# Transposing softmax weights as f16 pairs in 32-bit elements, with a new start and a new order of all steps

## The chip, the cores and the metric

The kernel runs on one core of one Trainium2 chip. The metric is the device time of one execution in microseconds (us), taken over several runs. Beside the runs there is one profiled execution, whose instructions the trace lists with start and duration.

## What is computed

There are 8 batches and 8 heads, x has 512 rows of 64 numbers in each, and a state has 32 rows. Two attentions go between x and the state, their outputs are put side by side over the heads (8 x 64 = 512 columns), and a two-layer network with a PReLU runs over all 4,352 rows.

```
scores = scale * x @ state.T          # 512 x 32 per batch and head
a      = softmax(scores, -1);  xread = a @ state
scores2 = scale * state @ x.T         # 32 x 512
a2     = softmax(scores2, -1); sread = a2 @ x
rows   = concat([xread, sread], axis=2) -> (8 * 544, 512)
h = rows @ w_in                       # 512 -> 2048
g = max(h, 0) + alpha * min(h, 0)
out = g @ w_out                       # 2048 -> 512
```

(The reference's network reads rows x w_in of shape 512 x 2048 and w_out of shape 2048 x 512.)

## The kernel before

The kernel does not compute xread and then multiply by w_in. For each batch it makes m = state x w_in (steps `m` and `mo`: TensorE into PSUM, then a cast to f16 by ScalarE or VectorE), and the first layer is then h = a x m, taken transposed: `first` (step `F`, line 570) runs for each of 16 slices `jc` of 128 columns of w_in two matmuls of 128 x 512, one for each group `g` of four heads. Stationary is m, moving are the softmax weights `aT`, which `weights(b, g)` cuts out.

The weights come about as follows, for each batch b. `sc` (line 328) gives the scores in PSUM with heads and states on the partitions. `sb` (line 360) turns them by a VectorE transpose of 32 x 32 blocks, so that the 32 states of a softmax lie next to each other in one partition. Then come `smax` (393), `ssh` (398, subtract the maximum, POOL for batches 1 to 7), `sexp` (407, ScalarE), `ssum` (416, 417, sum and reciprocal), `snorm` (420, multiply and write f16 into `an`, on VectorE for batches 2 to 7, on POOL for batches 0 and 1) and `wb` (428, VectorE transpose back from `an` to `aT`). Batch 0 goes another way, in two halves j, with TensorE transposes: `xt`/`xo` transpose x, `tsc` (367) gives the scores with tokens on the partitions, and `at`/`ao` transpose the weights.

The other softmax, over tokens, has steps `tm` (440), `nb` (447), `te` (457), `tsum` (467) and `tn` (473 on ScalarE, 475 on POOL: scale e by the sum's reciprocal), then `tt` (a transposing DMA issued by SyncE), and `rd` (494) reads x with it.

After `F` come `N` (623, ScalarE: the negative part) and `G` (626, VectorE: PReLU into g). The second layer of batch 0 is `S` (640). Batches 1 to 7, and the sread rows of all batches as an eighth, use a scheme of seven block products instead of eight: `U` (708, POOL) makes sums and differences of blocks of g, `W` (684, POOL) those of w_out once, `P` (729) multiplies, `K` (745) keeps an intermediate result, `Q` (760, 762) adds and stores.

What sets the order is the text `ORDER`: a list of some 1,100 steps written out, each a name of the table `steps` with its arguments, for instance `F.1.7.1` (first layer, batch 1, slice 7, PSUM bank 1) or `tn.0.1.p` (scale e of batch 0, group 1, on POOL). Each engine runs its own instructions in this order; semaphores keep the dependencies. PSUM has eight banks; the banks 0 to 5 are named by tags `k0` to `k5`, and a step that names a bank waits until the last reader of the tile before it is done.

`Z` (`fill`, line 246) multiplies a pattern by itself and reads no result: it keeps TensorE busy while it would wait. Its count is in units of 256 columns, and each fill takes a tile of its own in the named bank. A first fill of 16 units is issued outside the order, before the first step.

The start, outside the order too: ScalarE issues the load of batch 0's states (line 189), and `load_x0` issues the five loads of batch 0's x (line 176), three by SyncE and two by ScalarE; POOL writes the pattern, the identity for transposes and zeros into `st_pairs`. POOL issues all later loads of x (`lx`), of states (`lst`) and of the network's weights (`wi`, `wo`).

Of the kernel before, what the change touches and what calls it, by code (L numbers as in the profile page):

```python
# [9 lines left out]
F16 = mybir.dt.float16  # L10
EXP = mybir.ActivationFunctionType.Exp
# [11 lines left out]
xt.1.0.1.3 at.0.4 ao.0.a xo.1.0.0.v snorm.p.0.1 Z.1.3 xo.1.0.1.v oma.a xo.1.1.1.v at.1.1 sc.1 f.0.0.0.3 ao.1.a wi.2  # L23
F.0.3.0 F.0.2.2 m.0.1.4.1 mo.2.0.a.0 Z.5.3 n.0.0.0 f.0.0.1.5 N.0.3 mo.0.1.a.0 sb.1 tm.1 mo.0.1.a.1 F.0.7.4 F.0.5.1
N.0.2 g.0.0.0.1 g.0.0.0.0 G.0.2 n.0.0.1 G.0.3 g.0.0.1.1 nb.1.a te.1.0 g.0.0.1.0 N.0.7 N.0.5 F.0.6.3 G.0.7 smax.1
S.0.0.0.2 G.0.5 te.1.1 F.0.4.0 S.0.0.1 S.0.3.1.5 wo.1 wi.3 S.0.3.0 tsum.1 N.0.6 m.0.2 mo.0.2.a wo.2 S.0.1.1.4 wo.3
W.1.0.p G.0.6 S.0.1.0 m.1.1 F.0.10.1 N.0.4 G.0.4 mo.1.1.a N.0.10 G.0.10 F.0.8.3 S.0.1.3 S.0.1.2 ssh.p.1 sexp.1 F.0.9.0
ssum.1.s N.0.9 lx.2 xd.2 S.0.0.3 N.0.8 G.0.8 F.0.11.1 N.0.11 S.0.3.3 W.1.1.p snorm.p.1 m.0.3 mo.0.3.a S.0.3.2 S.0.0.2
G.0.11 sc.0.1 sc.0.0 F.0.15.3 G.0.9 F.0.14.1 S.0.3.4 S.0.1.4 S.0.1.5 tm.0 tn.1.1.a tn.1.0.a tt.1 N.0.15 G.0.15 W.2.0.p
N.0.14 G.0.14 wb.1 nb.0.a W.4.0.p F.0.13.0 te.0.1 te.0.0 tsum.0 F.0.12.3 N.0.12 S.0.0.5 S.0.1.7 m.1.3 F.1.7.1 N.0.13  # L30
tn.0.1.p W.3.1.p W.3.0.p tn.0.0.a N.1.7 G.0.12 G.0.13 G.1.7 F.1.3.3 N.1.3 W.2.1.p S.0.0.7 mo.1.3.a S.0.1.6 O.0.1.v
W.4.1.p F.1.5.0 N.1.5 S.0.3.6 G.1.3 G.1.5 F.1.2.1 N.1.2 G.1.2 F.1.15.4 N.1.15 F.1.12.3 G.1.15 N.1.12 G.1.12 m.1.2
F.1.6.0 N.1.6 G.1.6 F.1.14.1 N.1.14 G.1.14 mo.1.2.a S.0.0.4 S.0.0.6 O.0.0.a F.1.0.4 N.1.0 F.1.13.3 sc.2 sb.2 m.2.2.0.1
mo.2.2.a.0 mo.2.2.a.1 tm.2 S.0.3.7 tt.0 smax.2 S.0.3.5 O.0.3.a N.1.13 S.0.2.1.2 nb.2.a S.0.2.5 te.2.1 S.0.2.6 S.0.2.7
te.2.0 F.1.1.0 N.1.1 G.1.13 F.1.8.1 N.1.8 G.1.0 G.1.1 F.1.4.5 S.0.2.2 m.3.2 G.1.8 N.1.4 G.1.4 rd.0.3 rd.1.4 F.1.10.0
lst.1 ssh.p.2 sexp.2 rdo.1.a mo.3.2.a ssum.2.1 tsum.2 S.0.2.4 S.0.2.0 F.1.9.5 lx.3 P.1.2.0.1.4 snorm.v.2 rdo.0.a N.1.9
G.1.9 S.0.2.3 N.1.10 P.1.1.0.1.3 P.1.1.1.1 P.1.2.1.1 O.0.2.a tn.2.0.a m.2.3.1.2 mo.2.3.a.0 m.2.1 mo.2.3.a.1 wb.2
G.1.10 F.1.11.5 N.1.11 mo.2.1.a G.1.11 P.1.1.1.0 U.1.1.1.p str.1.1 sro.1.v tn.2.1.p tt.2 F.2.15.2 F.2.1.0 xd.3
# [24 lines left out]
K.3.4.a nb.6.a te.6.0 F.4.0.0 N.4.0 U.3.3.1.p F.4.1.2 N.4.1 mo.6.3.a.0 P.3.3.0.1 te.6.1 P.3.7.1.0 U.3.4.0.p P.3.7.1.1
xd.7 smax.6 ssh.p.5 G.4.6 P.3.7.0.1 P.3.3.1.0 sexp.5 P.3.2.1.1.1 P.3.2.0.0 G.4.0 m.5.2 m.6.2.5.0 mo.6.2.a.1 ssh.p.6
sexp.6 mo.5.2.a U.4.1.1.p P.3.2.0.1 P.3.2.1.0 G.4.1 Q.3.1.1 ssum.5.2 Q.3.0.0 snorm.v.5 P.3.4.1.1 P.3.4.1.0 P.3.3.1.1
P.4.1.0.0.0 mo.6.2.a.0 P.3.3.0.0 Q.3.0.1.a P.4.1.0.1 P.4.1.1.1 P.3.4.0.0 P.4.1.1.0 wb.5 K.4.1.a m.7.2.1.5 mo.7.2.a.0
mo.7.2.a.1 m.5.1 tsum.6 P.4.2.1.0.3 mo.5.1.a P.4.2.1.1 ssum.6.2 P.3.4.0.1 Q.3.1.0 snorm.v.6 F.5.15.1 F.5.3.5 N.5.3
P.4.2.0.1 P.4.2.0.0 N.5.15 G.5.3 F.5.2.4 N.5.2 U.4.1.0.p U.4.2.0.p sc.7 G.5.15 F.5.0.2 N.5.0 G.5.2 G.5.0 F.5.7.5 N.5.7
G.5.7 U.4.2.1.p P.4.6.0.1 F.5.12.1 N.5.12 G.5.12 F.5.5.4 U.4.3.0.p F.5.9.2 N.5.5 G.5.5 N.5.9 G.5.9 P.4.6.1.1 F.5.10.5
P.4.6.0.0 tm.7 P.4.6.1.0 F.5.8.1 N.5.10 F.5.1.4 F.5.14.2 K.4.2.a N.5.14 Q.4.0.0 G.5.14 P.4.5.1.1 U.4.3.1.p P.4.5.1.0  # L70
P.4.5.0.0 G.5.10 nb.7.a wb.6 te.7.0 P.4.5.0.1 N.5.1 te.7.1 tsum.7 F.5.4.3 G.5.1 N.5.8 G.5.8 P.4.7.0.0.2 F.5.11.5
N.5.11 G.5.11 K.4.4.a tn.7.0.a P.4.7.0.1 P.4.7.1.1 P.4.7.1.0 F.5.6.4 N.5.6 U.4.4.1.p P.4.3.0.1 P.4.3.1.1 tn.6.1.p
F.6.2.1 N.6.2 U.4.4.0.p P.4.3.0.0 P.5.1.1.0.5 P.4.3.1.0 sb.7 Q.4.1.1 P.4.4.1.1 P.4.4.0.1 G.6.2 G.5.6 smax.7 P.4.4.0.0
P.4.4.1.0 tn.6.0.a Q.4.0.1.a Q.4.1.0 N.5.4 G.5.4 F.6.4.1 N.6.4 G.6.4 P.5.1.0.0 F.6.9.0 F.6.1.4 N.6.9 G.6.9 F.5.13.2
N.5.13 tt.6 tn.7.1.p G.5.13 F.6.5.3 N.6.5 G.6.5 U.5.1.0.p P.5.1.1.1 F.6.14.1 P.5.1.0.1 U.5.2.0.p ssh.p.7 F.6.3.0
F.6.12.2 N.6.14 G.6.14 P.5.2.0.1.3 P.5.2.1.1 tt.7 F.6.6.1 K.5.1.a P.5.6.0.0 P.5.6.1.0 P.5.2.1.0 N.6.3 G.6.3 N.6.1
# [25 lines left out]
def kernel(  # L102
# [56 lines left out]
    def load_x(b):  # L159
# [4 lines left out]
        )  # L164


    def load_x0():
        xgs[0] = att.tile([128, H, 2, 2, D], F16, name="xg_0", tag="xg", bufs=3)
        for j in range(2):
            t = att.tile([128, H, 2, D], F32, name=f"x0_{j}", tag="ts", bufs=2)  # L170
            x0s.append(t)
# [642 lines left out]
```

## Time and profile before

| | us |
|---|---|
| median of 3 runs | 209.11 |
| lowest and highest run | 208.97, 209.56 |
| span of the profiled execution, first to last instruction | 209.0 |

The time of the profiled execution as a whole is not listed apart from its span.

In the profile PE is TensorE's matmuls, PEld its loads of stationary operands, DVE VectorE, ACT ScalarE, POOL GpSimd and SP SyncE. A row of the grouped view has line, engine, operation, the tiles written and read, shapes and count; then the busy time of the group in us, the mean of one in ns, the idle time of the engine just ahead of them and what ended it. A row of a timeline begins with start and duration in us. In the view by stretches each row is one stretch of time; behind its bounds and its length stand busy us and the number of instructions for PE, PEld, DVE, ACT and POOL, then TensorE's granted clock as a share, the mean number of DMA engines' busy share and GB/s. A row of waits says who waited for what, the us in total, how often, and the longest. The chain of waits is the work that ended last, followed back from the last instruction. Matmuls are pipelined, and their ends are modelled.

### The profile page before, as it was taken

What the parts mean: (1) busy time and instruction counts of PE and PEld (TensorE: products, weight loads), DVE (VectorE), ACT (ScalarE), POOL (GpSimd) and SP (SyncE); (2) the same over time, 40 slices, a digit from 0 to 9 for tenths busy, and PEclk for the clock granted to TensorE, in tenths of its full rate; (3) what the DMA queues carried; (4) which work ended last, traced back from release to release, by engine and by line L of the source; (5) the groups of instructions that cost most, each with busy time, mean ns of one, the idle gap of its engine ahead of it and who ended that gap; (6) DMA issues with size and microseconds to landing.
All of it is one profiled execution on the core that took longest, in us unless ns stands there. A gap on an engine that the chain in (4) does not pass through costs nothing.

```text
span 209.0 us, 5033 instructions
## 1 busy us (share of the span) xinstructions
PE 201.8 (97%) x1997; PEld 134.8 (65%) x1997; DVE 171.7 (82%) x251; ACT 155.6 (74%) x306; POOL 179.7 (86%) x113
## 2 busy tenths in 40 slices
PE   7899999998999999999999999999999999999992
PEld 2554343345556666678667765786877687788882
DVE  0688989999899999999999999999996967733231
ACT  4489999999999999987989968868855757603120
POOL 8149589987999899997997999887997999999960
PEclk9999999999999999999999999999999999999999
DMA  6999997984956799219886630126101200023223
GB/s 170 215 204 161 193 205 102 201 117 85 198 133 74 125 184 174 53 11 161 231 122 86 153 118 32 53 78 174 51 4 52 84 18 3 0 100 104 100 75 126
DMA packets 44038, 23.68 MB, mean 113 GB/s; under 512 B 22256, under 2 KB 43504, under 8 KB 44016
## 3 DMA queue, kind: packets, MB, share of 16 engines
q1 hardware_dynamic: 31152, 14.82, 28.3%
q0 software_dynamic: 11792, 8.09, 27.5%
q10 hardware_dynamic: 1072, 0.46, 0.9%
q8 instruction: 15, 0.25, 0.5%
q14 instruction: 7, 0.06, 0.1%
HBM read 17.31 MB, written 8.91 MB: 125 GB/s over the span
## 4 chain that ended last, share of the span: by engine, by line
PE 78%; DMA 7%; POOL 6%; ACT 4%; DVE 2%; issue 1%; SPq 0%; POOLq 0%
PE px L729 24%; PE h L570 21%; PE pv L729 13%; PE py L729 6%; POOL ws L684 5%; PE m_ps L521 4%; PE h L579 3%; DMA e2T<-e 2%; DMA xT<-xg 2%; DMA x<-in_x_dram 2%; PE fill L246 2%; PE sr_ps L494 2%; PE o L640 1%; ACT m L545 1%; POOL an L420 1%; PE sc L328 1%
## 5 line engine op out<-in xcount | busy, mean ns | idle before, releaser
L626 DVE SCALAR_TENSOR_TENSOR g<-neg,oma_sb,h 128x512 f16<-128x512 f32 (+1 forms) x142 | 93.9, 709 | 11.9 <-ACT neg L623 11.4
L623 ACT ACTIVATE neg<-h 128x512 f32<-128x512 f32 (+1 forms) x142 | 75.7, 580 | 16.6 <-PE h L570 11.5
L570 PE MATMUL h<-aT,m 128*128 128x512 f16 x252 | 66.8, 379 | 0.1
L729 PEld LDWEIGHTS <-gsum 128*128 128x128 f16 x480 | 46.6, 98 | 13.0 <-issue 0.9
L729 PEld LDWEIGHTS <-g 128*128 128x128 f16 x360 | 34.9, 98 | 9.0 <-issue 1.4
L708 POOL TENSOR_TENSOR gsum<-g,g 128x1024 f16<-128x1024 f16 (+1 forms) x16 | 32.2, 2012 | 5.5 <-DVE g L626 3.7
L570 PEld LDWEIGHTS <-m 128*128 128x128 f16 x252 | 23.8, 98 | 18.1 <-issue 1.8
L708 POOL TENSOR_TENSOR gsum<-g,gsum 128x1024 f16<-128x1024 f16 (+1 forms) x16 | 32.1, 2008 | 1.5 <-PE px L729 1.0
L708 POOL TENSOR_TENSOR gsum<-gsum,g 128x1024 f16<-128x1024 f16 (+1 forms) x16 | 32.1, 2009 | 1.0
L729 PE MATMUL px<-ws,gsum 128*128 128x256 f16 x240 | 32.1, 273 | 0.0
L708 POOL TENSOR_TENSOR gsum<-g 128x1024 f16<-128x1024 f16 (+1 forms) x16 | 32.0, 2011 | 0.0
L745 ACT COPY kept<-px 128x512 f32<-128x512 f32 (+1 forms) x24 | 13.6, 567 | 21.0 <-PE px L729 20.9
L547 ACT CAST m<-m_ps 128x512 f16<-128x512 f32 x35 | 19.2, 602 | 1.8 <-PE m_ps L521 1.5
L762 DVE TENSOR_TENSOR oq<-pv,kept 128x512 f32<-128x512 f32 (+1 forms) x16 | 10.4, 649 | 10.6 <-PE pv L729 10.4
L398 POOL TENSOR_TENSOR ts<-ts,mx 128x1024 f32<-128x1024 f32 x7 | 13.3, 1912 | 5.3 <-DVE mx L393 5.3
L729 PE MATMUL px<-w_out_sb,gsum 128*128 128x256 f16 x120 | 17.2, 273 | 0.0
L729 PE MATMUL px<-w_out_sb,g 128*128 128x256 f16 x120 | 17.2, 273 | 0.0
L729 PE MATMUL py<-w_out_sb,g 128*128 128x256 f16 x120 | 16.6, 273 | 0.0
L640 PE MATMUL o<-w_out_sb,g 128*128 128x512 f16 x64 | 16.4, 379 | 0.0
L729 PE MATMUL pv<-ws,gsum 128*128 128x256 f16 x120 | 16.4, 273 | 0.0
L729 PE MATMUL pv<-ws,g 128*128 128x256 f16 x120 | 15.9, 273 | 0.0
L545 ACT CAST m<-m_ps 128x1024 f16<-128x1024 f32 x13 | 13.3, 1023 | 0.4 <-PE m_ps L521 0.3
(75 smaller groups left out, 241.3 us busy)
## 6 DMA issues: line engine op xcount, KB each, us to landing
out_dram<-oq SPq DMA_DIRECT2D x28, 256.0 KB, 2.6
xg<-in_x_dram POOLq DMA_DIRECT2D x7, 512.0 KB, 7.0
w_in_sb<-in_moe_w_in_dram POOLq DMA_DIRECT2D x4, 512.0 KB, 8.5
w_out_sb<-in_moe_w_out_dram POOLq DMA_DIRECT2D x4, 512.0 KB, 12.9
out_dram<-osb SPq DMA_DIRECT2D x4, 256.0 KB, 3.5
x<-in_x_dram SPq DMA_DIRECT2D x2, 256.0 KB, 3.9
out_dram<-oq SPq DMA_DIRECT2D x4, 128.0 KB, 2.1
x<-in_x_dram ACTq DMA_DIRECT2D x1, 256.0 KB, 4.7
```

Of the source, the lines that this page charges most:

```text
L398: engine(e).tensor_tensor(blocks(cols(live["ts", b], j, S)), blocks(scored(b, j)), over_blocks(cols(live["mx", b], j, S // N)), ALU.subtract,)
L545: copier(e)(m_tile(b, f), t)
L547: copier(e)(m_tile(b, f)[:, g, :], t[g])
L570: nc.tensor.matmul(h.rearrange("p (r j s) -> p r j s", r=2, j=2), ms[b, f][:, g, 128 * j : 128 * (j + 1)], weights(b, g), start=(g == 0), ...
L623: nc.scalar.activation(neg, h, RELU, bias=0.0, scale=-1.0)
L626: nc.vector.scalar_tensor_tensor(g_tile(b, jc), negs.pop((b, jc)), oma_sb[:, jc : jc + 1], hs.pop((b, jc)), ALU.mult, ALU.add,)
L640: nc.tensor.matmul(outs[b, q], g_tile(b, jc)[:, 128 * q : 128 * (q + 1)], w_out_sb[:, jc, :], start=not begun and jc == 2 * jc2, stop=left ...
L684: engine(e).tensor_tensor(ws[i][:, rows, :], w_halves[a][:, rows, :], (ws[b] if b in ws else w_halves[b])[:, rows, :], ALU.subtract,)
L708: engine(e).tensor_tensor(t, x(), y(), op)
L729: nc.tensor.matmul(pbanks[b, name][:, i, :], of(b, c)[:, j, 128 * i : 128 * (i + 1)], moving[:, 4 * c + j, :], start=not begun and j == 0, ...
L745: copier(e)(t, pbanks[b, "x"])
L762: nc.vector.tensor_tensor(osb, pbanks[b, name], kept[b, add], ALU.add)
```

## The change

1. `state_norm` writes `an` for batches 1 to 7 so that the two weights that lie 512 apart in the old order (r = 0 and 1) become neighbours, and `weights_back` reads and writes the tiles as 32-bit elements: one VectorE transpose of 128 x 512 elements of 4 bytes instead of 128 x 1024 of 2 bytes. `weights` then hands `first` every second f16.
2. The x of batch 0 is loaded by four DMAs of 256 KB, all issued by SyncE; ScalarE issues only the load of the first states. These loads, the pattern (128 columns wide instead of 256), the identity and the zeros of `st_pairs` become steps of the order: `dx`, `dst`, `io`, `id`, `mz`.
3. All fills write into one tile in bank 5 and count in units of 128 columns. There are 133 units, the first 36 ahead of the first transposes.
4. `ORDER` is written anew. Some steps change engines: of the scalings `tn`, 10 instead of 5 are on POOL; 7 of 24 copies `K` are on VectorE instead of ScalarE; likewise 3 of `nb`, 2 of `rdo`, one `ao`.

```diff
 ORDER = """
-lst.0 cx.0.1.v cx.0.0.a xt.0.0.0.0 stc.a stt.1 cx.1.0.v sbd.1.a sto.a sbd.0.a xt.0.0.1.2 xt.0.1.0.3 xo.0.1.0.a
-xo.0.0.0.v Z.4.3 xo.0.0.1.v tsc.0.1.4 cx.1.1.v tsc.0.0 smax.0.0 ssh.v.0.0 xt.0.1.1.5 xo.0.1.1.a sexp.0.0 tsc.1.0.0
-Z.1.9 tsc.1.1 str.0.1 wi.0 m.0.0.2.3 sro.0.a Z.5.6 smax.0.1 ssh.v.0.1 Z.5.6 m.2.0.5.4 lx.1 sexp.0.1 m.1.0 mo.0.0.a.0
-la mo.0.0.a.1 ssum.0.0 wi.1 mo.1.0.a ssum.0.1 wo.0 mo.2.0.v.1 snorm.p.0.0 xt.1.1.0.0 xt.1.0.0.1 xt.1.1.1.2 xo.1.1.0.a
...
+dx.0.1.s dx.0.0.s dx.1.1.s io cx.0.1.v dx.1.0.s lst.0 Z.5.36 dst.a id xt.0.0.1.3 cx.0.0.a stc.v stt.4 xt.0.0.0.0
+Z.5.11 cx.1.1.v Z.5.3 mz xo.0.0.0.v sbd.0.a xo.0.0.1.a xt.0.1.1.0 sbd.1.v cx.1.0.a tsc.0.0.1 tsc.0.1 Z.5.8 smax.0.0 la
+xt.0.1.0.3 sto.a xo.0.1.1.a Z.5.3 xo.0.1.0.v str.0.2 wi.0 tsc.1.0.3 lx.1 tsc.1.1 ssh.v.0.0 Z.5.5 Z.5.4 sro.0.a Z.5.9
+smax.0.1 m.0.0.1.4 m.2.0.2.0 sexp.0.0 m.1.0 ssh.v.0.1 mo.0.0.a.0 sexp.0.1 Z.5.4 ssum.0.0 wi.1 Z.5.26 wo.0 xt.1.1.0.1
+mo.0.0.a.1 mo.1.0.a xt.1.0.0.4 xo.1.1.0.a xt.1.0.1.3 mo.2.0.v.1 ssum.0.1 xt.1.1.1.0 wi.2 xo.1.0.1.a Z.5.5 mo.2.0.a.0
...
 """
...
-        for e, j, first, last in (
-            (nc.sync, 0, 0, 4), (nc.sync, 0, 4, 8), (nc.scalar, 1, 0, 4),
-            (nc.scalar, 1, 4, 6), (nc.sync, 1, 6, 8),
-        ):
-            e.dma_start(
-                x0s[j][:, first:last, :, :],
-                x[0, first:last, 256 * j : 256 * (j + 1), :].rearrange("k (p r) d -> p k r d", r=2),
-            )
...
+    def load_x0(j, g, e):
+        heads = slice(4 * g, 4 * g + 4)
+        issuer(e).dma_start(
+            x0s[j][:, heads, :, :],
+            x[0, heads, 256 * j : 256 * (j + 1), :].rearrange("k (p r) d -> p k r d", r=2),
+        )
...
     def fill(k, n):
-        t = single(k, f"fill_{len(zs)}", [128, 512], F32)
-        zs.append(t)
-        widths = [384] * 2 if n == 3 else [512] * (n // 2) + [256] * (n % 2)
-        for w in widths:
+        if "fill" not in live:
+            live["fill"] = single(k, "fill", [128, 512], F32)
+        for w in [4] * (n // 4) + ([n % 4] if n % 4 else []):
             nc.tensor.matmul(
...
-            )
-
-    zs = []
-    fill(0, 16)
...
     def state_norm(e, b, j=None):
-        engine(e).tensor_tensor(
-            blocks(cols(live["an", b], j, S)),
-            blocks(cols(live["ts", b], j, S)),
-            over_blocks(cols(live["r1", b], j, S // N)),
-            ALU.mult,
-        )
+        an = blocks(cols(live["an", b], j, S))
+        ts = blocks(cols(live["ts", b], j, S))
+        r1 = over_blocks(cols(live["r1", b], j, S // N))
+        if b:
+            an = live["an", b].rearrange("p (a n r) -> p r a n", n=N, r=2)
+            ts = ts.rearrange("p (r a) n -> p r a n", r=2)
+            r1 = r1.rearrange("p (r a) n -> p r a n", r=2)
+        engine(e).tensor_tensor(an, ts, r1, ALU.mult)

     def weights_back(b):
-        nc.vector.transpose(live["aT", b], live["an", b])
+        nc.vector.transpose(live["aT", b].bitcast(U32), live["an", b].bitcast(U32))

     def weights(b, g):
         if b == 0:
             aT = live["aT", b].rearrange("p (j r g s) -> p r j g s", j=2, r=2, g=2)
         else:
-            aT = live["aT", b].rearrange("p (r j g s) -> p r j g s", j=2, r=2, g=2)
+            aT = live["aT", b].rearrange("p (j g s r) -> p r j g s", j=2, r=2, g=2)
         return aT[:, :, :, g, :]
```

More of the change, by code (lines that the diff above doesn't have):

```diff
@@ L10 @@
 F16 = mybir.dt.float16
+U32 = mybir.dt.uint32
 EXP = mybir.ActivationFunctionType.Exp
@@ L24 @@
[L24 to L38, printed above, removed]
@@ L164, in load_x, with issuer @@
         )
[L167 to L171, printed above, removed]
-        for e, j, first, last in (
-            (nc.sync, 0, 0, 4), (nc.sync, 0, 4, 8), (nc.scalar, 1, 0, 4),
-            (nc.scalar, 1, 4, 6), (nc.sync, 1, 6, 8),
-        ):
-            e.dma_start(
-                x0s[j][:, first:last, :, :],
-                x[0, first:last, 256 * j : 256 * (j + 1), :].rearrange("k (p r) d -> p k r d", r=2),
-            )
+    xgs[0] = att.tile([128, H, 2, 2, D], F16, name="xg_0", tag="xg", bufs=3)
+    for j in range(2):
+        t = att.tile([128, H, 2, D], F32, name=f"x0_{j}", tag="ts", bufs=2)
+        x0s.append(t)
+    def issuer(e):
+        return {"s": nc.sync, "a": nc.scalar, "p": nc.gpsimd}[e]
+    def load_x0(j, g, e):
[4 more added lines that the diff above has]
+        )
     def x0_cast(j, g, e):
@@ L200, in load_alpha, with write_pattern, write_identity @@
             )
-    pattern = consts.tile([128, 256], F16)
-    nc.gpsimd.iota(
-        pattern, pattern=[[37, 256]], base=-4800, channel_multiplier=29,
-        allow_small_or_imprecise_dtypes=True,
-    )
-    ident = consts.tile([128, 128], F16)
-    make_identity(nc, ident)
+    pattern = consts.tile([128, 128], F16)
+    ident = consts.tile([128, 128], F16)
+    def write_pattern():
+        nc.gpsimd.iota(
+            pattern, pattern=[[37, 128]], base=-4200, channel_multiplier=29,
+            allow_small_or_imprecise_dtypes=True,
+        )
+    def write_identity():
+        make_identity(nc, ident)
     st = consts.tile([128, n_j, D], F16)
@@ L238, with clear_pairs @@
     st_pairs = consts.tile([128, H, 2, N], F16)
[L239 removed]
+    def clear_pairs():
+        nc.gpsimd.memset(st_pairs, 0.0)
     def fill(k, n):
[L242 to L245 removed]
+        if "fill" not in live:
+            live["fill"] = single(k, "fill", [128, 512], F32)
+        for w in [4] * (n // 4) + ([n % 4] if n % 4 else []):
             nc.tensor.matmul(
[L247 to L253 removed]
+                live["fill"][:, : 128 * w].rearrange("p (a c) -> p a c", c=128), pattern,
+                pattern.unsqueeze(1).to_broadcast([128, w, 128]),
+                start=True, stop=True, skip_group_check=True,
+            )
     stT = consts.tile([128, B * H * N], F16)
```

144 lines of the change are left out of this document (78 added, 66 removed).

## The prediction

> **What bounds the kernel now.** I read the busy totals first, then engine use by stretches.
>
> ```profile
> span 209.0 us, 5033 instructions
> PE 201.8 (97%) x1997; PEld 134.8 (65%) x1997; DVE 171.7 (82%) x251; ACT 155.6 (74%) x306; POOL 179.7 (86%) x113
> ...
> 0.00:5.00 5.00, 3.61 (x9) 1.08 (x10) 0.00 (x0) 2.06 (x3) 4.28 (x13) 1.00 0.62 165
> 5.00:17.00 12.00, 11.20 (x135) 6.76 (x136) 8.95 (x19) 8.24 (x17) 4.73 (x7) 1.00 1.29 210
> 17.00:35.00 18.00, 17.52 (x142) 7.05 (x141) 16.79 (x26) 17.61 (x36) 14.87 (x10) 1.00 1.14 177
> 35.00:60.00 25.00, 24.31 (x260) 12.46 (x259) 23.80 (x33) 23.76 (x45) 22.94 (x15) 1.00 0.83 142
> 60.00:150.00 90.00, 89.91 (x999) 62.62 (x998) 88.27 (x121) 79.22 (x158) 83.13 (x45) 1.00 0.54 109
> 150.00:200.00 50.00, 50.00 (x416) 40.41 (x414) 31.67 (x52) 23.55 (x51) 47.69 (x27) 1.00 0.16 54
> 200.00:209.00 9.00, 5.25 (x49) 4.47 (x46) 2.22 (x5) 1.12 (x3) 2.06 (x2) 0.94 0.33 117
> ```
>
> From 60 to 200 us TensorE is busy 139.91 of 140: nothing done to another engine can shorten this by itself. VectorE, with 88.27 of 90 up to 150, is nearly as full; the half-size transposes give it slack, not the program time. What can move is TensorE's time outside the program's matmuls: 0.80 + 0.48 + 0.69 + 0.09 = 2.06 us not busy between 5 and 150, the start, the tail (from 205.3 on), and the fills, which count as busy and compute nothing:
>
> ```profile
> L246 PE MATMUL fill<-pattern 128*128 128x512 f16 x18 | 6.6, 513 | 1.3 <-POOL pattern L203 1.2
> L246 PE MATMUL fill<-pattern 128*128 128x384 f16 x6 | 1.8, 394 | 0.0
> L246 PE MATMUL fill<-pattern 128*128 128x256 f16 x1 | 0.3, 273 | 0.0
> ...
> 1.24 3.60 PE L246 MATMUL fill<-pattern 128*128 128x512 f16 x8 [1.24 <-POOL pattern L203]
> 9.26 1.49 PE L246 MATMUL fill<-pattern 128*128 128x512 f16 x5
> ...
> 98.26 1.73 PE h L570 x8
> ```
>
> The busy times overlap, so the chain's row gives the step: 8 matmuls of 512 columns in 1.73 us, 0.216 each. The first fills took 3.60/8 = 0.45, though the granted clock reads 1.00 there; those at 9.26 took 0.30. Fills before: 18 x 512 + 6 x 384 + 256 = 11,776 columns, of which 4,096 ahead of the first transposes and 7,680 among work.
>
> **The change, part by part.**
>
> *First x by SyncE alone.* Five loads on two queues become four of 256 KB on one.
>
> ```profile
> 0.74 1.60 SPq L176 DMA_DIRECT2D x<-in_x_dram  x3
> x<-in_x_dram SPq DMA_DIRECT2D x2, 256.0 KB, 3.9
> 4.22 0.62 ACT L182 CAST xg<-x 128x512 f16<-128x512 f32 x1 [0.47 <-DMA x<-in_x_dram]
> 5.61 1.07 DVE L182 CAST xg<-x 128x512 f16<-128x512 f32 x2 [5.61 <-DMA x<-in_x_dram]
> 8.85 0.69 DVE L393 TENSOR_REDUCE mx<-tsc 128x16 f32<-128x512 f32 x1 [1.04 <-PE tsc L367]
> ```
>
> An issue costs 1.60/3 = 0.53, so the fourth is issued by 0.74 + 4 x 0.53 = 2.86. Both quarters of the first half of x go ahead of everything else on this queue: the first is there at about 4.2 as now, the second at 1.27 + 3.9 = 5.2 instead of 5.6. Then follow a cast (0.62, on ScalarE), transposes, a copy and 14 new units of fill (1,792 columns: 1.6 us at 0.45 per 512, 0.76 at 0.216) before the first maximum at 8.85. Gain 0.4 with fast fills, a loss of 0.4 with slow ones if nothing else were late; as the fills have their own bank and the continuous matmuls begin earlier, I take 0.4 gained (bounds -0.7 to +0.4). Moved past on this queue: alpha's four small loads and the next x transpose, neither waited for here. POOL issues the first 112 KB of states ahead of the identity, and w_in's third part ahead of the first normalization, in a time in which it is idle. The Trainium skill, page Trainium Kernel Development and Optimization, Key Constraints, says that the queues of SP, ACT and POOL share the same 16 DMA engines and that several issuers save only issue time. By that rule the last quarter, issued 2.86 - 2.34 = 0.5 later, would be the whole cost; no run here shows it alone.
>
> *The start's order.* VectorE now evicts m (0.63) between the two row sums instead of after them, and copies the first batch's transposed weights in place of ScalarE.
>
> ```profile
> 13.95 0.63 DVE L547 CAST m<-m_ps 128x512 f16<-128x512 f32 x1
> ...
> 34.70 1.26 PE L570 MATMUL h<-aT,m 128*128 128x512 f16 x4
> PEld L570 <- DVE aT L428: 0.3, 1, 0.3
> ```
>
> The second normalization, and with it the first full matmuls of batch 0, waits behind that eviction: between 0 and 0.63 lost; half, +0.3.
>
> *Transposes of pairs and their feed.*
>
> ```profile
> L428 DVE STREAM_TRANSPOSE aT<-an 128x1024 f16<-128x1024 f16 x7 | 8.7, 1237 | 0.0
> L360 DVE STREAM_TRANSPOSE ts<-sc 128x1024 f32<-128x1024 f32 x7 | 8.7, 1244 | 0.8 <-PE sc L328 0.8
> L286 DVE STREAM_TRANSPOSE alpha_sb<-alpha_rows 128x32 f32<-128x32 f32 x1 | 0.2, 202 | 0.0
> L420 DVE TENSOR_TENSOR an<-ts,r 128x1024 f16<-128x1024 f32 x6 | 7.3, 1213 | 0.1
> L420 POOL TENSOR_TENSOR an<-ts,r 128x1024 f16<-128x1024 f32 x1 | 1.9, 1915 | 0.5 <-DVE r L417 0.5
> L505 ACT CAST XS<-sr_ps 128x128 f16<-128x128 f32 x8 | 3.3, 489 | 0.2 <-PE sr_ps L494 0.2
> L268 ACT CAST st<-st 128x128 f16<-128x128 f32 x1 | 0.3, 293 | 0.0
> ```
>
> 1,024 elements cost the same in 2 and in 4 bytes, so elements count: (1,237 - 202)/992 = 1.043 ns each, and 512 cost 202 + 480 x 1.043 = 0.70 us. That is 0.53 saved seven times, 3.7 on VectorE. The normalization now writes every second f16. No VectorE row shows this; the nearest, ScalarE's cast into every fourth element, takes 489 ns against 293 for a dense one, 1.53 ns more per element, 1.57 us for 1,024. Bounds 0 to +1.57 each; I take 0, since at 1,213/1,024 = 1.18 ns per element VectorE writes one at a time already.
>
> TensorE then reads the weights as moving operand at every second element: 2 x 16 x 7 = 224 matmuls. No row has this; bounds 0 and one more pass, 0.216 each, 48 us. I take 0. The Trainium skill, page Advanced Engine Details and Errata, Memory Cachelines, says that SBUF lines have 16 bytes and that two hits in a line keep full speed; a step of 4 bytes has four hits. By this rule too the sum has 0; the trace cannot check it.
>
> For batch 1 the transpose sits on the path: its first matmuls wait for it at 34.70. The 0.53 come off there. Ahead of them ScalarE, busy 17.61 of 18 in this stretch, loses one scaling of e, one small multiply and the copy of weights:
>
> ```profile
> L473 ACT ACTIVATE e<-e,r 128x512 f16<-128x512 f16 x11 | 7.8, 722 | 0.6 <-DVE r L467 0.6
> L475 POOL TENSOR_SCALAR e<-e,r 128x512 f16<-128x512 f16 x5 | 3.5, 696 | 0.3 <-DVE r L467 0.3
> L745 ACT COPY kept<-px 128x512 f32<-128x512 f32 x21 | 12.5, 595 | 14.5 <-PE px L729 14.4
> L658 DVE COPY osb<-o 128x512 f32<-128x512 f32 x1 | 0.7, 692 | 0.1
> ```
>
> Only 0.48 of TensorE idleness is left in that stretch, so more than 0.5 can't be had: -0.5 (bounds 0 and -1.0, the second with the time hidden in modelled ends of matmuls).
>
> *Moved steps after 35 us.* Five scalings of e go to POOL (5 x 0.70 = 3.5, beside sums that take 83.13 of 90), seven copies of kept to VectorE (7 x 0.69 = 4.8, all from batch 5 on, where it is busy 31.67 of 50). Queued behind a scaling on POOL are sums of g for the products; if these sums came too late, the 3.5 would reach TensorE. I cost both at 0: the sums stand, by their place in the order, as far ahead of their products as before. The six other transposes free 3.2 us of VectorE. The idle time there to be won is 0.69 + 0.09, in waits such as
>
> ```profile
> PE sr_ps L494 <- DMA e2T<-e: 0.6, 1, 0.6
> PEld L328 <- DMA xT<-xg: 0.6, 1, 0.6
> ```
>
> I take -0.3 (bounds -0.8 and +1.0, as new places can make waits too).
>
> *The tail.* After the last product come, as now, one sum on VectorE and its store, but a copy of batch 7 with a store of 256 KB moves in just ahead of them: +0.1 (0 to +0.3).
>
> ```profile
> 205.29 0.42 DVE L762 TENSOR_TENSOR oq<-pv,kept 128x256 f32<-128x256 f32 x1 [1.27 <-PE pv L729]
> ```
>
> Sum: -0.4 + 0.3 - 0.5 - 0.3 + 0.1 = -0.8 against the profiled span of 209.0. What lies around the span isn't listed; the lowest run is 208.97, the median 209.11, 0.1 above the span. So 209.0 - 0.8 + 0.1 = 208.3.
>
> **The rivals.**
>
> A, *fills that outlast the waits* (slower). The new fills have 133 units of 128 = 17,024 columns, 4,608 first and 12,416 among work: 4,736 more than now, 9.25 x 0.216 = 2.0 us of TensorE in strict order. They cost nothing where TensorE would wait anyway. For it: the stretch 5 to 17 has only 0.80 idle on top of the present fills. Against: modelled ends hide waiting, and 3,328 of the columns stand in one place, before the transposes of batch 1's x, where the scores' chain is waited for. It decides once operands are ready before their fill ends; then 209.0 - 0.8 + 2.0 + 0.1 = 210.3.
>
> B, *the start gains much more*: all idle time between 5 and 150 goes. -0.4 + 0.3 - 2.06 + 0.1 = -2.1, hence 207.0. For it: lighter ScalarE in the stage where it is full. Against: the DMA waits quoted are not touched by lighter engines.
>
> C, *nothing reaches the end*: the transposes ease VectorE only, the start is as long as it was. 209.1.
>
> D, *the strided writes cost what ScalarE's row says*: six normalizations on VectorE at +1.57 - 0.53 = +1.04, one at +1.9 on POOL by doubling, on engines that are 98% and 92% full: up to 6.2 + 1.9 = 8, of which half might reach TensorE: 213.
>
> E, *the strided reads halve TensorE's rate*: 209 + 48 = 257; the change would then not do what it says. Nothing in the trace speaks for it.
>
> **How the numbers follow.** Forecast 0.36, A 0.21, B 0.17, C 0.17, D 0.06, E 0.03. The measurement tells 0.3% (0.63 us) from no change. The forecast's own range, 207.6 to 208.9, is faster by that in 0.28 of its 0.36; B is faster throughout and C in 0.02: 0.47. Same: 0.08 of the forecast, 0.13 of C, 0.01 of A: 0.22. Slower: 0.20 of A, 0.02 of C, D and E: 0.31. The range leaves out D and E and the ends of A and B: 206.7 to 210.9.
>
> **What would show it.** The transposes at 0.70 us and normalizations at 1.21; eight matmuls of batch 1 or later still in 1.73; the first maximum at about 8.4 and the first matmuls of batch 1 at 34.2 or earlier; 60 to 200 as full as now. A first maximum after 8.85 or batch 1 after 34.9 would make the forecast wrong, as would a row of waits for POOL's sums on TensorE.

## The result and the profile after

The changed kernel takes 217.55 us (median of 5 runs; 217.08 the lowest) against 209.11 for the kernel before: a ratio of 1.0391 [1.0371, 1.0412]. It is 8.4 us slower, where 0.8 us less was forecast. Some executions take 3 to 4 us longer than the others of the same kernel (two of these five, one of them the profiled one, with 221.45 us and a span of 219.3), so ratios are taken without them, the profile's rows are read for places and durations, and the sums below are made from run times. A ratio stands with its 95% interval in brackets.

First the stretches, columns as before:

```profile
5.00:17.00 12.00, 11.80 (x153) 6.92 (x153) 9.31 (x21) 9.45 (x19) 5.96 (x8) 1.00 1.26 206
17.00:35.00 18.00, 17.58 (x139) 7.54 (x138) 17.21 (x27) 17.05 (x33) 16.00 (x12) 1.00 1.17 189
35.00:60.00 25.00, 25.00 (x297) 12.50 (x295) 24.11 (x34) 22.69 (x44) 22.89 (x15) 1.00 0.92 141
60.00:150.00 90.00, 82.83 (x828) 54.81 (x826) 84.71 (x111) 70.00 (x136) 76.62 (x42) 0.98 0.48 97
150.00:200.00 50.00, 50.00 (x457) 38.35 (x455) 38.98 (x62) 25.77 (x51) 44.19 (x23) 1.00 0.17 54
```

Up to 60 us TensorE is as full as it was, fills included. From 60 to 150 it is busy 82.83 of 90 where it had 89.91: 7.17 us idle, at a granted clock of 0.98. The waits of TensorE there, and the chain, name two places:

```profile
PE h L580 <- DVE g L636: 5.2, 3, 3.3
PE sc L336 <- DMA xT<-xg: 2.0, 1, 2.0
```

```profile
54.96 8.11 DMA xT<-xg
63.74 1.91 PE h L580 x8
...
82.31 4.20 DVE nb L459
86.51 2.64 DVE g L636 x4
89.19 2.72 PE h L580 x6
```

The first place is VectorE's small multiply, nb times the scale, which the change moved from ScalarE for batches 0, 4 and 6: two elements per partition. The groups by shape, with busy us and the mean ns:

```profile
L580 PE MATMUL h<-aT,m 128*128 128x512 f16 x252 | 72.0, 392 | 5.3 <-DVE g L636 5.2
...
L435 DVE TENSOR_TENSOR an<-ts,r 128x1024 f16<-128x1024 f32 x6 | 8.1, 1350 | 0.1
L459 DVE TENSOR_SCALAR nb<-nb 128x2 f32<-128x2 f32 x3 | 8.0, 2657 | 0.0
L438 DVE STREAM_TRANSPOSE aT<-an 128x512 uint32<-128x512 uint32 x7 | 4.9, 707 | 0.0
...
L457 ACT ACTIVATE nb<-nb 128x2 f32<-128x2 f32 x5 | 1.2, 236 | 0.1
```

The same multiply takes ScalarE 236 ns and VectorE 2,657, while a reciprocal of the same size takes VectorE 0.15 us. The timeline around the worst of the three shows what it is held by:

```profile
80.93 2.12 POOL L718 TENSOR_TENSOR gsum<-g 128x1024 f16<-128x1024 f16 x1
...
82.23 4.27 DVE L459 TENSOR_SCALAR nb<-nb 128x2 f32<-128x2 f32 x1
...
83.05 1.35 POOL L485 TENSOR_SCALAR e<-e,r 128x512 f16<-128x512 f16 x2
84.38 2.11 POOL L718 TENSOR_TENSOR gsum<-g 128x1024 f16<-128x1024 f16 x1
86.42 3.37 DVE L636 SCALAR_TENSOR_TENSOR g<-neg,oma_sb,h 128x512 f16<-128x512 f32 x5
87.87 4.03 PE L580 MATMUL h<-aT,m 128*128 128x512 f16 x10 [3.26 <-DVE g L636]
```

It begins at 82.23 while GpSimd works and ends at 86.50, which is where GpSimd's run of back-to-back instructions ends (84.38 + 2.11 = 86.49). The other two end with an instruction of GpSimd as well: at 31.75, where one ends at 31.73, and at 120.80, where one ends at 120.76. The five sums that make g stand behind it on VectorE, and TensorE waits 3.26 us for them. After that stall ten matmuls take 4.03 us, 0.40 each in place of 0.216, and the row of the granted clock shows one slice at 6 there:

```profile
PEclk9999999999999999699999999999999999999999
```

The second place is the scores of batch 3, which wait for the DMA transposes of its x. In the kernel before (its second profile, below) the load of batch 4's x is issued at 61.10 us, after these scores:

```profile
52.62 3.56 SPq L305 DMA_TRANSPOSE xT<-xg  x1
...
59.38 0.41 PE L328 MATMUL sc<-xT,stT 64*32 64x256 f16 x16
...
61.10 0.95 POOL L161 DMA_DIRECT2D xg<-in_x_dram  x1
```

Now GpSimd issues it at 52.69, ahead of the transposes, which then take 8.11 us, where the median of the six DMA transposes of x is 4.4:

```profile
xT<-xg SPq DMA_TRANSPOSE x6, 4.4
...
48.28 0.97 POOL L163 DMA_DIRECT2D xg<-in_x_dram  x1 [0.93 <-PE sr_ps L504]
52.69 0.95 POOL L163 DMA_DIRECT2D xg<-in_x_dram  x1
54.96 1.79 SPq L313 DMA_TRANSPOSE xT<-xg  x1
...
63.12 0.41 PE L336 MATMUL sc<-xT,stT 64*32 64x256 f16 x16 [2.00 <-DMA xT<-xg]
```

### The profile page after: what moved, and what is told of

The parts are those of the page before. It is cut to its first block, busy times and chain, and to the rows that moved or that the text cites. A ratio compares the mean times of both kernels' runs of the same rounds, so it can differ in the third digit from the quotient of the medians.

```text
span 219.3 us, 5070 instructions
## 1 busy us (share of the span) xinstructions
PE 206.4 (94%) x2011; PEld 134.7 (61%) x2011; DVE 182.7 (83%) x265; ACT 148.0 (67%) x285; POOL 182.7 (83%) x118
## 4 chain that ended last, share of the span: by engine, by line
PE 71%; DVE 13%; DMA 9%; issue 3%; ACT 1%; POOL 1%; SPq 0%; ACTq 0%; POOLq 0%
PE h L580 20%; PE px L739 20%; PE pv L739 11%; PE py L739 5%; DVE g L636 5%; DMA xT<-xg 4%; PE h L589 3%; DMA xg<-in_x_dram 3%; PE m_ps L531 3%; DVE nb L459 3%; DMA x<-in_x_dram 2%; PE o L650 2%; DVE nb L450 2%; PE fill L257 2%; DVE ts L368 2%
## 5 line engine op out<-in xcount | busy, mean ns | idle before, releaser
L636 DVE SCALAR_TENSOR_TENSOR g<-neg,oma_sb,h 128x512 f16<-128x512 f32 (+1 forms) x142 | 95.3, 710 | 13.4 <-ACT neg L633 12.6
L633 ACT ACTIVATE neg<-h 128x512 f32<-128x512 f32 (+1 forms) x142 | 77.1, 582 | 36.6 <-PE h L580 21.6
L580 PE MATMUL h<-aT,m 128*128 128x512 f16 x252 | 72.0, 392 | 5.3 <-DVE g L636 5.2
L406 POOL TENSOR_TENSOR ts<-ts,mx 128x1024 f32<-128x1024 f32 x7 | 13.4, 1915 | 9.8 <-DVE mx L401 5.3
L557 ACT CAST m<-m_ps 128x512 f16<-128x512 f32 x31 | 17.4, 596 | 5.7 <-PE m_ps L531 5.6
L739 PE MATMUL py<-w_out_sb,g 128*128 128x256 f16 x120 | 17.5, 272 | 0.0
L650 PE MATMUL o<-w_out_sb,g 128*128 128x512 f16 x64 | 17.1, 379 | 0.0
L555 ACT CAST m<-m_ps 128x1024 f16<-128x1024 f32 x15 | 15.4, 1026 | 2.0 <-PE m_ps L531 1.9
L755 ACT COPY kept<-px 128x512 f32<-128x512 f32 (+1 forms) x17 | 9.7, 571 | 10.1 <-PE px L739 5.8
L739 PE MATMUL px<-w_out_sb,gsum 128*128 128x256 f16 x120 | 15.9, 273 | 0.0
```

The source lines that it names most:

```text
L406: engine(e).tensor_tensor(blocks(cols(live["ts", b], j, S)), blocks(scored(b, j)), over_blocks(cols(live["mx", b], j, S // N)), ALU.subtract,)
L555: copier(e)(m_tile(b, f), t)
L557: copier(e)(m_tile(b, f)[:, g, :], t[g])
L580: nc.tensor.matmul(h.rearrange("p (r j s) -> p r j s", r=2, j=2), ms[b, f][:, g, 128 * j : 128 * (j + 1)], weights(b, g), start=(g == 0), ...
L633: nc.scalar.activation(neg, h, RELU, bias=0.0, scale=-1.0)
L636: nc.vector.scalar_tensor_tensor(g_tile(b, jc), negs.pop((b, jc)), oma_sb[:, jc : jc + 1], hs.pop((b, jc)), ALU.mult, ALU.add,)
```

## The experiments

Each is set against runs of the kernel before on the same chip. Their median is 209.18 us beside the small multiplies back on ScalarE, the same move alone and the two dense variants; 208.91 beside the pairs in the old order and the fills; 209.46 beside the single elements, the new start and its reverse, and the load moved too far; 209.31 beside the last three.

**The small multiplies back on ScalarE**, and as a cross-check the same move alone in the kernel before.

```
-... nb.0.v ... nb.4.v ... nb.6.v ...
+... nb.0.a ... nb.4.a ... nb.6.a ...
```

> The changed kernel with the three small multiplies nb of batches 0, 4 and 6 back on ScalarE, all else as changed. Held-multiply theory (the multiply of 128 x 2 on VectorE ends only when POOL is between two instructions, and holds all that is queued on VectorE): the row of multiplies on VectorE, 8.0 us for three, is gone, TensorE's idle stretches of 3.3 and 1.5 us near 84 and 119 go with the slow matmuls after them, and the time falls from 217.5 by 5 to 7 us to 210.5 to 212.5. New-order theory (the new places cost the time, the multiplies only stand where there is a wait anyway): 216 to 217.5. Strided-read theory (the step of two elements in the moving operand costs TensorE all of the difference): 217, with eight h matmuls still at 1.9 us.

213.69 us, a ratio of 1.0193 [1.0133, 1.0254]: 3.8 us come back, but not all that the theory of the held multiply expected. TensorE is busy 88.39 of 90 between 60 and 150. In the 3.8 us a lower clock has its part: all five runs of the changed kernel have a mean granted clock of 0.987 to 0.991, the four of this one 1.000.

```
-... nb.0.a ... nb.4.a ... nb.6.a ...
+... nb.0.v ... nb.4.v ... nb.6.v ...
```

> The kernel before with one thing changed: the three small multiplies nb of batches 0, 4 and 6 on VectorE instead of ScalarE. Held-multiply theory: each lasts until POOL pauses, 1 to 4 us instead of 0.2, and the time rises by 1.5 to 6 us to 210.5 to 215. New-order theory: 209.1, multiplies of 0.15 to 0.3 us.

215.61 us, 1.029 [1.0217, 1.0364]: 6.4 us for three multiplies of 128x2, without anything else of the change. No run took that time: two with a mean granted clock of 1.000 took 214.44 and 214.48 us, two with 0.991 and 0.992 took 216.78 and 216.75. The profile is of one of the latter. The three multiplies, with durations min/median/max, and the timeline around the first:

```profile
L449 DVE TENSOR_SCALAR nb<-nb x3: 157/955/1539, 33.1 to 117.9; 128x2 f32<-128x2 f32 x3
```

```profile
29.74 4.33 POOL L684 TENSOR_TENSOR ws<-w_out_sb,ws 128x1024 f16<-128x1024 f16 x2
31.98 1.24 DVE L428 STREAM_TRANSPOSE aT<-an 128x1024 f16<-128x1024 f16 x1
33.14 0.95 DVE L449 TENSOR_SCALAR nb<-nb 128x2 f32<-128x2 f32 x1
34.13 0.69 ACT L457 ACTIVATE e<-sc,nb 128x512 f16<-128x512 f32 x1 [3.38 <-DVE nb L449]
...
35.62 0.41 PE L521 MATMUL m_ps<-w_in_sb,stT 64*32 64x512 f16 x8 [2.62 <-ACT e L457]
```

Here two things add up. The multiply stands behind a transposition on VectorE's queue (31.98 to 33.2), and then is held until GpSimd's pair of sums ends at 34.07. ScalarE, with its exponentials waiting for nb, stands still for 3.38 us, and TensorE for 2.62. The third multiply, of two elements like the others, begins at 117.89, while GpSimd runs nothing (from 116.93 to 118.12), and takes 0.16 us: it is GpSimd's work that holds the other two.

**The same multiply, one element at a time.** This separates being held from being queued.

```
-            nc.vector.tensor_scalar_mul(nb, nb, -scale)
+            for g in range(2):
+                nc.vector.tensor_scalar_mul(nb[:, g : g + 1], nb[:, g : g + 1], -scale)
```

> The kernel before with the small multiplies of batches 0, 4 and 6 on VectorE as in the run that took 215.61 us, but each as two multiplies of one element per partition in place of one of two. Theory that what is held is the mode in which VectorE takes both halves of an operand at once through the port it shares with GpSimd, which one element cannot use: no multiply over 0.3 us, 208.8 to 209.6. Rival, that any multiply of VectorE with source and target in SBUF is held while GpSimd works: up to 2.1 us for each, as before or worse, 215 to 219.

213.42 us. The view by line, with durations min/median/max:

```profile
L450 DVE TENSOR_SCALAR nb<-nb x6: 113/142/144, 33.1 to 113.8; 128x1 f32<-128x1 f32 x6
```

None of the six is held, at 0.14 us each beside the same GpSimd work. The time falls by only 2.2 us and stays far above the 208.8 to 209.6 expected: the multiply starts at 33.1 as before, and ScalarE still waits for it (3.8 us in two places). So of the 6.4 us in the old order roughly 2 go with the hold, and 4 stay with the multiply's place in VectorE's queue. The split is rough, as the intervals of the two ratios overlap (1.0185 [1.0102, 1.0268] here), and for the new order no run makes it. The Trainium skill, page SBUF — State Buffer, section "SBUF: two separate sides" with its part "Who interferes with whom", says that VectorE and GpSimd share one pair of ports, which an instruction locks for its whole length; VectorE needs it for its modes with two ports, and tensor_scalar may enter them. The six free multiplies of one element agree with that rule, as do the ends of the held ones. A wait for the one instruction that holds the ports would have ended at 83.05 in the changed kernel, though, and not at 86.49; how the two engines take turns no run shows.

**Dense weights and full transposes**, the pairs taken out of the changed kernel: alone, and with the multiplies on ScalarE.

```
-        nc.vector.transpose(live["aT", b].bitcast(U32), live["an", b].bitcast(U32))
+        nc.vector.transpose(live["aT", b], live["an", b])
...
-            aT = live["aT", b].rearrange("p (j g s r) -> p r j g s", j=2, r=2, g=2)
+            aT = live["aT", b].rearrange("p (r j g s) -> p r j g s", j=2, r=2, g=2)
```

> The changed kernel with the transposes, the normalizations and the weights as before (f16, 128 x 1024, dense moving operand), the small multiplies left on VectorE. Strided-read theory with the size read from the profile: eight h matmuls go from 1.91 to 1.73 us, 224 of them by 2.2 us in all; normalizations from 1.35 to 1.21 us, transposes back from 0.71 to 1.24; the time falls by 1 to 2.5 us, to 215 to 216.5. If the stride is hidden: 217.5, and more if the longer transposes of VectorE reach TensorE (up to 3.7 us more). Held-multiply theory: the held multiplies stay, so no more than the stride's 2.2 is gained.

216.88 us, from a single run of four (the other three took 221.29 to 221.65), 0.7 below the changed kernel's median: the pairs are not the bulk of the loss.

> Both edits: small multiplies on ScalarE and transposes, normalizations and weights as before, in the new order. Held-multiply and strided-read theories together: 208.5 to 210, that is, near the kernel before. New-order theory: 214 or more.

213.02 us, 1.0172 [1.0122, 1.0222]. That missed: with the same transposes as before and the multiplies where they were, 3.8 us stay. They belong to the order, the start or the fills, or to what else changed its engine.

**The kernel before, profiled again.**

> The kernel before, unchanged, for a second profile. The profiled execution shown at first has a span of 209.0 us, while the runs beside the other experiments have spans of 206.9 to 207.3 with times of 208.8 to 209.3. If the first profile was an ordinary one, this one has a span of 209.0 too; if it was a long one, this one has 206.9 to 207.3, with fewer idle gaps of TensorE between 35 and 60 us or a shorter tail, and it is the one to compare with.

208.6 us with a span of 206.7. The first profile, with 209.0, was thus of an execution 2 us longer than the ordinary ones, and the time stands 1.9 us above the span. It lost them early: the scores of batch 1 begin at 15.95 us there and at 14.35 here, those of batch 3 at 61.68 and 59.38, and from then on the two profiles stay 2.3 us apart. In this one TensorE has no idle time at all from 60 to 150:

```profile
60.00:150.00 90.00, 90.00 (x948) 62.92 (x946) 88.18 (x120) 78.61 (x156) 83.19 (x45) 1.00 0.54 110
```

**The pairs alone in the old order**, first as the change has them, then with TensorE reading neighbouring elements and VectorE putting the columns right when it makes g.

> The kernel before with the pairs alone: the normalization writes every second f16, the transposes are of 512 elements, TensorE reads the weights of batches 1 to 7 at every second element; order, start and fills as before. Theory of the strided read: 224 matmuls at 0.0096 us more each, 2.1 us, less 0 to 0.5 us for batch 1 on the path: 210.7 to 211.3. Theory that the modelled row of 8 matmuls (1.91 us against 1.73) only spreads waiting: 208.6 to 209.2.

```
-                    h.rearrange("p (r j s) -> p r j s", r=2, j=2),
+                    h.rearrange("p (r j s) -> p r j s", r=2, j=2) if b == 0 else h.rearrange("p (j m) -> p j m", j=2),
...
-                    weights(b, g),
+                    weights(b, g) if b == 0 else live["aT", b].rearrange("p (j g m) -> p j g m", j=2, g=2)[:, :, g, :],
...
+            out = out.rearrange("p (r m) -> p r m", r=2)
+            neg, h = (t.rearrange("p (m r) -> p r m", r=2) for t in (neg, h))
```

> As the run with the pairs alone, but TensorE reads 2 x 256 neighbouring elements of the weights, so that h comes out with its columns in the order (half, token, pair member), and the sum on VectorE that makes g reads h and neg at every second element and writes g dense. Theory of the strided read: the 2.1 us are gone, 8 matmuls take 1.73 us again, and 208.5 to 209.3 results, if VectorE's sums cost no more for reading at a step of two; if they cost 0.1 us more each (112 of them, 11 us on an engine that is 97% full from 35 to 150 us), above 212.

210.61 us, 1.0093 [1.006, 1.0126], for the first, and 208.99, 1.0009 [0.9975, 1.0043], for the second: 1.7 us for the read at every second element, and nothing for the rest of the pairs. In the chains, the row that took 1.73 in the kernel before; then the group of these matmuls. With the pairs as the change has them:

```profile
98.49 1.80 PE h L573 x8
```

```profile
L573 PE MATMUL h<-aT,m 128*128 128x512 f16 x252 | 68.8, 386 | 0.1
```

With neighbouring reads:

```profile
95.98 1.73 PE h L573 x8
```

```profile
L633 DVE SCALAR_TENSOR_TENSOR g<-neg,oma_sb,h 128x512 f16<-128x512 f32 x126 | 87.7, 742 | 9.1 <-ACT neg L626 8.7
...
L573 PE MATMUL h<-aT,m 128*128 128x512 f16 x252 | 66.7, 379 | 0.1
```

The strided read costs (1.80 - 1.73)/8 = 0.009 us for each matmul, 4%, 2.0 us for 224 of them. VectorE's sums read h and neg at a step of two for nothing: 742 ns, against 741 in the second profile of the kernel before.

**Fills taken out.** From the variant at 213.02 us, 50 of its 97 units among the work.

```
-xt.1.1.1.0 wi.2 xo.1.0.1.a Z.5.5 mo.2.0.a.0
+xt.1.1.1.0 wi.2 xo.1.0.1.a mo.2.0.a.0
...
-f.0.0.0.1 m.0.1.3.4 F.0.3.0 Z.5.7 Z.5.1 wo.3 n.0.0.0 F.0.2.2 Z.5.8
+f.0.0.0.1 m.0.1.3.4 F.0.3.0 wo.3 n.0.0.0 F.0.2.2
```

> The changed kernel with the three small multiplies on ScalarE, dense weights and transposes as before (213.02 us as measured), and 50 of the 97 units of fill among the work left out: those after the third part of the first states' and x's products, behind the transposes of batch 1's x and in the stretch of the first matmuls of batch 0. Theory of rival A, that the fills outlast the waits: 50 x 0.054 = 2.7 us less, 210.3. Theory that the fills only stand where TensorE would wait and the new order itself costs the 3.8 us: 212.6 to 213.4.

214.38 us against 213.02, above what either theory gave: nothing saved. TensorE's idle time in the early stretches grew instead, to 12.00 - 9.77 = 2.23 and 0.94 us:

```profile
5.00:17.00 12.00, 9.77 (x142) 5.94 (x141) 9.38 (x20) 9.37 (x18) 6.68 (x10) 1.00 1.26 211
17.00:35.00 18.00, 17.06 (x133) 7.12 (x134) 16.49 (x26) 17.16 (x34) 15.39 (x11) 1.00 1.15 184
```

The fills stand where TensorE waits, as the forecast had it, and rival A falls.

**New start with the old rest, and the reverse.** The order is cut at the first matmul of batch 1; both have dense weights and the multiplies on ScalarE.

> The order of the changed kernel up to the first matmul of batch 1 (its x loads, fills, start and engines), all later steps in the order and on the engines of the kernel before; small multiplies on ScalarE, dense weights. By the work done on TensorE the run with the whole new order is 1.0 us behind at 35 us and 3.5 at 150: theory that start and later places each bring their part, 209.6 to 210.4 here. Theory that all of the 3.8 us grows from the start: 212.4 or more. Theory that the start is no worse: 208.6 to 209.2.

209.51 us, 1.0006 [0.9978, 1.0034]: between the two lower forecasts, and not to be told from the kernel before.

> The other way round: start, loads and fills of the kernel before up to the first matmul of batch 1, all later steps in the new order and on the new engines, small multiplies on ScalarE, dense weights. Theory that each brings its part: 208.9 + 2.5 to 3.0, so 211.2 to 212.1. Theory that all grows from the start: 208.6 to 209.5. Theory that it is all in the later places: 212.4 to 213.2.

214.47 us, 1.022 [1.0147, 1.0292], above all three forecasts; three of its four runs have a mean granted clock of 0.992, and the one at 1.000 took 212.54, inside the last of them. Start, loads and fills cost nothing that can be measured; what is left lies in the places and engines after 35 us. The one large wait in that run is again the scores of batch 3:

```profile
63.17 0.41 PE L328 MATMUL sc<-xT,stT 64*32 64x256 f16 x16 [2.58 <-DMA xT<-xg]
```

**The load of batch 4's x moved**, first too far, then to the middle, in the variant at 213.02 us.

```
-... P.1.2.1.0 lx.4 mo.3.0.v.1 ...
+... G.2.2 sc.3 lx.4 G.2.0 ...
```

> The changed kernel with the small multiplies on ScalarE and dense weights (213.02 us), and one step moved: the load of batch 4's x (512 KB, issued by GpSimd at 52.84 us in that run) is put behind the scores of batch 3, about where the kernel before has it (61.10). Theory of the collision: that load delays the DMA transposes of batch 3's x, for which TensorE waits 1.0 us at 62 us; without it the wait goes, 211.7 to 212.1. Rival: batch 3's x is itself late, because the reads of batch 0 that free its buffer come 1.7 us later than before (47.45 against 45.71): the wait stays, 212.6 to 213.4.

214.78 us, slower, and yet it tells: the scores of batch 3 no longer wait, but the load, queued behind GpSimd's sums, leaves only at 65.39, and now batch 4's scores wait. Their transposes collide in turn: they are issued at 71.27, after the load of batch 5's x at 70.30, and take 8.5 us.

```profile
79.84 0.41 PE L337 MATMUL sc<-xT,stT 64*32 64x256 f16 x16 [3.04 <-DMA xT<-xg]
```

```
-... P.1.2.1.0 lx.4 mo.3.0.v.1 ...
+... rd.2.2 N.2.2 lx.4 U.1.2.0.p ...
```

> The changed kernel with the small multiplies on ScalarE and dense weights (213.02 us), and the load of batch 4's x put in the middle: ahead of the sum U.1.2.0, so that GpSimd issues it at about 59 us, behind the transposes of batch 3's x (issued at 55 to 56) and well ahead of those of batch 4's. Theory of the collision: neither batch's scores wait for DMA, and 1.0 to 1.6 us go: 211.4 to 212.0. Rival, that batch 3's x is late because its own load comes 1.7 us later than before: TensorE waits at 62 us as it did, 212.6 to 213.4.

211.72 us, 1.0116 [1.0072, 1.016]: 1.3 us less, as the theory of the collision had it. The interval overlaps that of the variant without the move, so it is the trace that shows the cause. The load now leaves after the transposes, and the scores follow with no wait, although batch 3's own load is no earlier than it was (49.02, against 48.43 in the variant without the move):

```profile
49.02 0.97 POOL L164 DMA_DIRECT2D xg<-in_x_dram  x1 [0.88 <-PE sr_ps L501]
56.23 1.32 SPq L314 DMA_TRANSPOSE xT<-xg  x1
59.67 0.95 POOL L164 DMA_DIRECT2D xg<-in_x_dram  x1
...
61.78 0.40 PE L337 MATMUL sc<-xT,stT 64*32 64x256 f16 x16
```

**All three mended together**: the new order with its pairs, the multiplies on ScalarE, the load in the middle, neighbouring reads.

> The changed kernel with three things mended together: the small multiplies on ScalarE, the load of batch 4's x in the middle, and the pairs kept but read by TensorE as neighbouring elements. If the three causes add up: 217.5 - 3.8 for the multiplies - 1.3 for the load - 1.7 for the read = 210.7, between 210.0 and 211.4; what is left over 208.9 then belongs to other new places after 35 us. If one of them only covers another, 212 or more.

210.07 us, 1.004 [1.0024, 1.0055]. The three causes add up: 7.5 of the 8.4 us are gone. The remaining 0.8 us lie in other new places or engines, the ten scalings on GpSimd and the seven copies on VectorE among them, which no run took apart.

The sum hides something. In the run before (211.72) TensorE reads neighbours as well, from dense weights, and this run differs from it by the pairs alone; yet it is 1.65 us quicker, and the two intervals do not overlap. So in the new order the pairs, once TensorE reads neighbours, are worth about that, where in the old order they were worth nothing (208.99 against 208.91). It fits that the pairs with the strided read, taken out of the new order, gave back only 0.7 us and not 1.7. The other new places cost 2.4 us without the pairs then (211.72 against 209.31), and 0.8 with them. Two waits of TensorE for VectorE, 0.4 us for g and 0.2 for aT, are in the earlier trace and not in this one; the rest is not traced to a place.

**The parts that cost nothing, together**: new start, pairs with neighbouring reads, old order after that.

> The new start (loads, fills, order and engines up to the first matmul of batch 1), the pairs with neighbouring reads, and all later steps in the order and on the engines of the kernel before. Theory that TensorE is full behind the start and only the start can give time: 208.3 to 209.5, the same as before. Rival, that the shorter transposes take 0.5 us off the first matmuls of batch 1, as forecast: 207.9 to 208.4.

209.38 us, 1.0016 [0.9999, 1.0034]. No version tried is shown to be faster than the kernel before.

## Why the prediction was wrong

The step that failed is "moved steps after 35 us". It counted five scalings and seven copies, costed "both at 0", and took -0.3 for the whole. The small multiply appears in it only under the transposes, as work that ScalarE "loses"; what VectorE would pay for it was not asked. It cost 3.8 us, the largest part, held by GpSimd's work and itself holding what is queued behind it on VectorE. The step's own bound of +1.0 for new waits was too narrow as well: the load of batch 4's x, moved ahead of batch 3's transposes, cost 1.3 (2.0 us of waiting in the profile); the forecast had followed DMAs past their queues for the first x only. What the scalings and the copies cost, for which the step had its two zeros, no run shows by itself.

The strided read of TensorE was named with bounds of 0 and 0.216 each and taken at 0. The mechanism was seen and the size was off: 0.009 each, 1.7 us in runs. The rule of the Trainium skill's page Advanced Engine Details and Errata, Memory Cachelines, by which the forecast let a step of 4 bytes cost nothing, differs from the measurement, and the measurement decides.

Right were the transposes at 0.70 us (707 ns), elements and not bytes setting their price, and the start: forecast -0.1 with its order, shown as 0 within 0.3%. The -0.5 for batch 1's shorter transposition did not come: the last run, with start and pairs, is at 209.38 and not below 208.4. The weights come earlier, and the first matmuls of batch 1 don't: behind the same new start they begin 18.97 us after that batch's scores with the short transposes and 18.98 without them. Rival C was right in this. The normalization costs 0.14 us more on VectorE (1,350 against 1,213), near the lower bound taken; in the old order nothing of it reaches the time.

Two signs that the forecast named were not broken, by luck. The first maximum was to come at about 8.4 and batch 1 at 34.2 or earlier; they came at 8.64 and 33.75, against 8.85 and 34.70 in the first profile. But in the second profile of the same unchanged kernel they come at 7.70 and 33.09, so these signs tell one execution from another and not the change. The signs that did fail were the right ones to name: eight matmuls at 1.91 us where 1.73 was said, normalizations at 1.35 where 1.21 was said, and TensorE idle between 60 and 150.

Rival A put the loss in the fills: fewer fills saved nothing. Rival D's 213 was nearest of all to the time, by accident: a strided write costs VectorE 0.14 us where it had 1.57, and GpSimd nothing (1,916 ns against 1,915). Rival E had the mechanism of the strided read, at 24 times the 0.009 us measured.

The base was off too. The span of 209.0 was read as 0.1 us below the median; it was of a longer execution, with 1.9 us around it. The idle 0.69 us between 35 and 60, from which the failed step hoped to win its 0.3, is not there in the second profile (25.00 busy of 25.00), nor are the 0.09 after it: in an ordinary execution that step had nothing to win, and a wait put there is paid in full.

## What to carry to other kernels

Before a step moves to VectorE, price it on VectorE, however small: look how many elements it has in a partition (two were held, one was not), what GpSimd runs beside it, and what is queued ahead of it and behind it. Where a load moves, look at which transfers it now runs into, and at the last one that TensorE waits for. Where TensorE is full, as in the old order, relief elsewhere was worth nothing and each new wait counts, at times with a lower clock after it. Profile the unchanged kernel twice before reading a fraction of a microsecond from its start.

## What the hardware showed that was not expected

- VectorE's multiply of two elements was not let in between GpSimd's back-to-back instructions: it waited from 82.23 to 86.50 us over the rest of one sum, two scalings and another sum. It was not always so: the one at 30.69 ended at 31.75, at the end of the instruction that ran, though the next began at 31.71. With one element it took 0.14 us, with two and GpSimd idle 0.16.
- A stall of TensorE of 3.3 us was followed by ten matmuls at 0.40 us each, at a granted clock of 0.63 from 88 to 92 us, so the stall cost more than its length. It was alike after 2.62 us in the old order with the multiplies on VectorE (0.65 from 36 to 40) and after 2.58 with the old start and the new rest (0.58 from 64 to 68), but not after 3.04 us in the run with the load moved too far, where the clock reads 1.00 throughout the 8 us that follow. What decides it, no run shows.
- TensorE reads f16 at a step of 4 bytes 4% slower than neighbours; VectorE reads f32 at a step of two for nothing, and writes f16 at a step of two 11% slower (1,350 against 1,213 ns); GpSimd writes so at no cost (1,916 against 1,915).
- DMA transposes of 512 KB took 8.1 us when another load of 512 KB had been issued 2.3 us before them, and 8.5 when it had been issued 1.0 us before; the median is 4.4, and with the load in the middle the longest is 5.0.
